# Features folded a second time on VectorE, and stage D in pairs of 64-row products: batches 2 to 7 of a Fourier and channel-mix kernel

## Chip, cores and metric

One core of a Trainium2 chip. The metric is the device time of one execution in microseconds (us); lower is better.

## What is computed

The input `x` has 8 batches of 3072 positions by 256 features, in float32.

```
X = fft over positions, then fft over features;  x = real part of X
x_prev = x one position earlier (zero at position 0)
xk = mu_k * x + (1 - mu_k) * x_prev
xr = mu_r * x + (1 - mu_r) * x_prev
k = relu(xk @ w_k) ** 2          # 256 -> 1024
r = sigmoid(xr @ w_r)            # 256 -> 256
out = r * (k @ w_v)              # 1024 -> 256, float32
```

## The kernel before

Everything is computed in float16 with float32 sums. A batch passes these stages.

- **Load and fold.** `load_xh` brings positions and mirrored positions into `xp` and `xm` (two halves h of a batch: 9 and 8 rows of 256 features on each partition). `fold` (L171, L173, VectorE) adds to each feature d the value at the mirrored place: `p`. `butterfly` (L182, VectorE) then adds and subtracts features 0 to 127 and 128 to 255 of `p`: `eo`, with an even part (e = 0) and an odd part (e = 1) of 128 features each.
- **Stage A** (`a_slots_0`, `a_half`; L553, L567): products of `eo` with a table of cosines and sines over part of the positions. The 48-row products come in pairs, one on the upper and one on the lower 64 rows of the array, and run side by side. Result `a`, features on partitions, copied from PSUM by ScalarE (L524).
- **Stage D** (`d_item`; L607): the transform over features. Each of 13 units takes two products of 128 rows and 128 columns (e = 0, 1) with the table `w_eo`; four units make an item, so a batch has three items of four units and one of one. The result goes to `g_all` by one copy for each item (`d_evac`, L524). `turned` (L630) multiplies column 128 of all units by a small table and writes it back.
- **Stage C** (`c_pairs`; L681): the rest of the transform over positions, in pairs of 64-row, 64-column products. Result `pq`. Four items a batch; in each batch the copy of the second one is made by VectorE (L522), the others by ScalarE.
- **Mixing** on VectorE: `halves` (L694) makes `y` from `pq`, `diff` (L702) the differences of neighbouring positions, `mix` (L714, L725) the inputs xk and xr.
- **Channel mix.** The positions of a batch are six chunks of 512. A chunk takes four steps. In each, `k_piece` makes four 512-column products (L760) and ScalarE the relu (L770, `rl`); every second step `square` (L780, VectorE) squares two steps' worth. `v_tile` (L801) multiplies with `w_v`, eight products a step, five steps behind the k products; its first four products read the square of the chunk's first half, its last four that of the second. `r_item` (L787, L792) comes once a chunk. `v_out` (L823, VectorE) multiplies by r, and SP's queue writes the result.

PSUM is six banks for three wide tiles (`ps_w`: psW, 1024 columns) and two for two narrow ones (`ps_v`: psV). Each wide product group takes the next of the three tiles in turn, and so must wait until the tile's last copy has been read out.

**Order.** The program is one list of 197 steps, written out by hand and pinned on every engine (`pin_order`). `at(step, ...)` puts work into a step, `event(step, ...)` puts a run of paired items right behind that step's v products. In a step PE issues the k products, the items of the step, the v products, and then the event. If an event has more than two items and does not begin with `a_slots_0`, the next step's v products are moved up to stand right behind it, ahead of the next step's k products (`early_v`, L925 to L930).

From step s0 = 24 b on (b = 0 to 5), batch t = b + 2 is prepared: folds and butterflies at s0 + 9 to 14, stage D items at s0 + 27, 29, 31 and 33, `turned` at s0 + 34, and three events at s0 + 37 (two C items and a stage A half item of batch t + 1), s0 + 41 (the same) and s0 + 45 (slot 0 and the last two stage A half items, which fill the two tiles that slot 0 has taken). For t = 7 there is no next batch and two events are left. A stretch below is one uninterrupted run of paired products. Batch 2's folds and butterflies stand earlier, at steps 17 to 21, beside the mixing of batch 1.

Of the kernel before, what the change touches and what calls it, by code (L numbers as in the profile page):

```python
# [10 lines left out]
FP16 = mybir.dt.float16  # L11
INT32 = mybir.dt.int32
UINT32 = mybir.dt.uint32
AF = mybir.ActivationFunctionType
ALU = mybir.AluOpType
# [5 lines left out]
def _v(ap, extra_offset, free_dims):  # L21
    new_ap = [list(ap.ap[0])] + [[s, c] for (s, c) in free_dims]
    return dataclasses.replace(ap, offset=ap.offset + extra_offset, ap=new_ap)
# [16 lines left out]
def kernel(  # L40
# [10 lines left out]
    nc = tc.nc  # L51

    B, S, D = x.shape
    F = moe_w_k.shape[1]
    P = 128
    N1, R = 48, 64
    NSL = 27
    NU = 26
    NJ, NJ1 = 14, 6

    const = ctx.enter_context(tc.tile_pool(name="const", bufs=1))
    p_pool = ctx.enter_context(tc.tile_pool(name="p", bufs=2))
    eo_pool = ctx.enter_context(tc.tile_pool(name="eo", bufs=2))
    y_pool = ctx.enter_context(tc.tile_pool(name="y_sb", bufs=1))
    mix_pool = ctx.enter_context(tc.tile_pool(name="mix", bufs=1))
# [7 lines left out]
    def ps_slot(kind, n, cols):  # L73
        k = ps_n[kind] % n
        ps_n[kind] += 1
        return psum.tile([P, cols], FP32, name=f"ps{kind}{k}", tag=f"ps{kind}{k}", bufs=1)

    def ps_w():
        return ps_slot("W", 3, 1024)
# [25 lines left out]
    xp_t, xm_t, p_t, eo_t = {}, {}, {}, {}  # L105
    V = nc.vector
# [2 lines left out]
    xp_sb = [const.tile([112, 9, 256], FP16, name=f"xp{n}") for n in range(3)]  # L109
    xm_00 = const.tile([96, 514], FP16)  # L110
    xp_00 = const.tile([96, 9, 256], FP16)
    xp_32 = const.tile([96, 5, 256], FP32)
    idx_4 = const.tile([96, 2], UINT32)
    idx_8 = const.tile([96, B, 2], UINT32)
# [10 lines left out]
    def parts(b):  # L125
        return 112 if b > 1 else 96
# [32 lines left out]
    def fold(b, h, q0=0, n=0):  # L159

        n = n or 9 - h
        if (b, h) not in p_t:
            p_t[b, h] = p_pool.tile([112, 9, 256], FP16, name="p")
        k = parts(b)
        p, xp, xm = p_t[b, h][0:k], xp_t[b, h][0:k], xm_t[b, h][0:k]
        o = XM0 + 256 * (8 - h - q0)
        if (b, h, q0) == (0, 0, 0):
            xm, o = xm_00, 1
        if (b, h) == (0, 0) and q0 < 5:
            xp = xp_32  # L170
        V.tensor_tensor(out=p[:, q0:q0 + n], in0=xp[:, q0:q0 + n],  # L171
                        in1=_v(xm, o + 256, [(-256, n), (-1, 256)]), op=ALU.add)
        V.tensor_tensor(out=p[:, q0:q0 + n, 0], in0=xp[:, q0:q0 + n, 0],  # L173
                          in1=_v(xm, o, [(-256, n)]), op=ALU.add)

    def butterfly(b, h, n=0):
        n = n or 9 - h
        eo_t[b, h] = eo_pool.tile([112, 9, 2, 128], FP16, name="eo")
        k = parts(b)
        p = p_t[b, h][0:k]  # L180
        for e in range(2):
            V.tensor_tensor(out=eo_t[b, h][0:k, 0:n, e], in0=p[:, 0:n, 0:128],  # L182
                            in1=p[:, 0:n, 128:256], op=ALU.subtract if e else ALU.add)
# [51 lines left out]
    for xm in xm_sb:  # L235
        V.memset(_v(xm, XM0 + 2048, [(256, 2)]), 0.0)
    V.memset(xm_00[:, 257:258], 0.0)
    iota = nc.gpsimd.iota
    def rows():
        for a in range(2):  # L240
# [7 lines left out]
    w_eo = const.tile([P, 2, 128], FP16)  # L248
    ramp = const.tile([P, P], INT32)
    row_i = const.tile([P, 4], UINT32)  # L250
    lo64, hi64 = slice(0, 64), slice(64, 128)
# [15 lines left out]
    g_all = const.tile([P, NU // 2, 256], FP16)  # L267
# [160 lines left out]
    def zero_rows():  # L428
        for n in (0, 2):
            nc.gpsimd.memset(xp_sb[n][32:64, 8], 0.0)  # L430
# [43 lines left out]
    def loads_2():  # L474
        for lo in (0, 64):
            k = slice(lo, 64 if lo == 0 else 112)
            iota(idx_g8[k], pattern=[[S // 8, B], [-1, 2]], base=S // 8 - 1 - lo // 16,
                 channel_multiplier=-8)
            iota(idx_g0[k], pattern=[[S, B]], base=S - lo // 2, channel_multiplier=-64)
        iota(idx_g0[0:1], pattern=[[S, B]], base=0, channel_multiplier=0)  # L480
        for a in range(2):
            gather(wk_sb[1][a], moe_w_k, row_i[:, 2 + a:3 + a])
        load_xh(1, 1)
        for a in range(2):
            gather(wr_sb[1][a], moe_w_r, row_i[:, 2 + a:3 + a])
        zero_rows()

    def eo_sine():
        nc.scalar.activation(out=w_eo.rearrange("p a b -> p (a b)"),
# [9 lines left out]
    def half_tables():  # L499
        ps = ps_w()  # L500
        turned(8, 13, ps, "")
        for o, w, step in ((512, 0, 2), (512, 1, 2), (512 + WB, WA, 1)):
            nc.tensor.matmul(out=ps[0:112, o:o + WB], lhsT=order[0:96, 0:112],
                             rhs=_v(w_pm[0:96], w, [(step, WB)]), start=w != 1, stop=w > 0)
        evac(_v(g_all, 256 * 8 + 128, [(256, 5)]), ps[:, 0:5], "A")
        V.tensor_copy(out=w_hh, in_=ps[0:112, 512:512 + 2 * WB])

    def eo_rest():

# [6 lines left out]
    a_t = {}  # L516
# [3 lines left out]
    def evac(out_ap, in_ap, eng):  # L520
        if eng == "V":
            V.tensor_copy(out=out_ap, in_=in_ap)  # L522
        else:
            nc.scalar.activation(out=out_ap, in_=in_ap, func=AF.Copy)  # L524
# [86 lines left out]
    def d_evac(ps, u0, n, bank, eng):  # L611
        evac(_v(g_all, 256 * u0, [(64, 2), (128, 2 * n), (1, 64)]),
             _v(ps, 0, [(bank, 2), (64, 2 * n), (1, 64)]), eng)

    def d_item(b, n, eng="A"):

        k = min(4, NU // 2 - 4 * n)
        ps = ps_w()
        d_units(b, ps, 4 * n, k, 512)
        d_evac(ps, 4 * n, k, 512, eng)  # L620

    def d_small(b, u, n, eng="A"):
        ps = ps_v()
# [223 lines left out]
    for a in range(2):  # L847
        nc.tensor.matmul(out=mu_ps[:, 2 * a:2 * a + 2], lhsT=mu_p[:, a], rhs=unit, start=True,
                         stop=True)
# [26 lines left out]
    w, first = ps_w(), ps_w()  # L876
# [15 lines left out]
    for a in range(2):  # L892
        t = x_t["t", a] = mix_pool.tile([P, 24, 64], FP16, name=f"t{a}")
        ts(t[:, 0:4], y[:, 0:4, a], mu_n[:, a, 0:1], MUL)
    for a in range(2):
        for z in range(2):
            V.scalar_tensor_tensor(out=_v(x_t[0, 0, 0], 1536 * a + 64 * z, [(128, 2), (1, 64)]),  # L897
                                   in0=_v(first, 512 + 64 * a - 384 * z, [(128, 2), (1, 64)]),
                                   scalar=mu_f[:, a, 0:1],
                                   in1=_v(x_t["t", a], 64 * z, [(128, 2), (1, 64)]),  # L900
                                   op0=ALU.mult, op1=ALU.add)
# [15 lines left out]
    work = {}  # L917

    def at(step, f, *args):
        work.setdefault((step, "x" if f in (a_item, a_sum, d_item, d_small, c_item, c_tiles, turned, minus_0, r_item) else "w"),  # L920
                        []).append((f, args))


# [3 lines left out]
    def event(step, *items):  # L927
        work.setdefault((step, "e"), []).extend((f[0], f[1:]) for f in items)
        if len(items) > 2 and items[0][0] is not a_slots_0:
            early_v.add(step + 1)  # L930
# [2 lines left out]
    nk = 4 * len(chunks)  # L933

    LAG, EARLY, SHORT = 5, 3, 3
    ES, EV = (37, 41, 45), "AVAAAAAA"
    OUT_FIRST = (12, 20, 28, 36, 38, 40)
    SQUARE_A = (6, 7, 8, 9)
    v_steps = {4 * n + tb + LAG: (c, tb) for n, c in enumerate(chunks) for tb in range(4)
# [61 lines left out]
    at(17, c_tiles, 1)  # L1001
    at(17, fold, 2, 0)
    event(18, (c_item, 1, 0, 8), (c_item, 1, 8, 8))
    at(18, butterfly, 2, 0)
    at(18, fold, 2, 1)
    event(20, (c_item, 1, 16, 8), (c_item, 1, 24, 4), (a_half, 2, 0, 0))
    at(19, diff, 1, 0, 12)
    at(20, r_item, (0, 1, 1))
    at(23, a_half, 2, 0, 1)
    at(20, mix, 1, 0, 0, 0, 0, 12)  # L1010
    at(21, butterfly, 2, 1)
    at(21, mix, 1, 0, 0, 1, 0, 12)
    at(22, diff, 1, 12, 26)
    at(21, load_gate)
# [6 lines left out]
    at(26, mix, 1, 0, 1, 0)  # L1021
    event(27, (a_slots_0, 2), (a_half, 2, 1, 0), (a_half, 2, 1, 1))
    at(28, r_item, (1, 0, 0))
    at(28, d_item, 2, 0)
    at(28, mix, 1, 0, 1, 1)
    at(29, d_item, 2, 1)
    at(30, mix, 1, 1, 1, 0)
    at(31, d_item, 2, 2)
    at(31, mix, 1, 1, 1, 1)
    at(32, r_item, (1, 0, 1))  # L1030
    at(33, d_item, 2, 3)
    at(34, turned, 0, 13)
    for n, c in enumerate(chunks[8:]):
        at(4 * n + 36, r_item, c)
    for b in range(B):
        s0 = 24 * b

        for n, st0 in enumerate((2, 4, 6, 8) if b > 1 else ()):
            at(s0 + st0, mix, b, n // 2, 1, n % 2)
        if b and b + 3 < B:  # L1040
            at(s0 + 22, load_gate)
            for h in range(2):
                at(s0 + 22, load_xh, b + 3, h)
        t = b + 2
        if t < B:
            if b:
                for n, st0 in enumerate((9, 10, 12, 14)):
                    at(s0 + st0, butterfly if n % 2 else fold, t, n // 2)
                for n, st0 in enumerate((27, 29, 31, 33)):
                    at(s0 + st0, d_item, t, n)  # L1050
                at(s0 + 34, turned, 0, 13)
            c = [(c_pairs, t, 8 * n, (8, 8, 8, 4)[n], EV[n]) for n in range(4)]
            if t + 1 < B:
                event(s0 + ES[0], c[0], c[1], (a_half, t + 1, 0, 0, EV[4]))
                event(s0 + ES[1], c[2], c[3], (a_half, t + 1, 0, 1, EV[5]))
                event(s0 + ES[2], (a_slots_0, t + 1), (a_half, t + 1, 1, 0, EV[6]), (a_half, t + 1, 1, 1, EV[7]))
            else:
                event(s0 + ES[0], *c[:2])
                event(s0 + ES[1], *c[2:])
        t = b + 1  # L1060
        if b and t < B:
            at(s0 + 16, halves, t, 0, 15)
            at(s0 + 18, halves, t, 15, 27)
            for a in range(2):
                at(s0 + 19 + a, diff, t, 0, 26, (a,))
                at(s0 + 21 + a, mix, t, 0, 0, a)
            at(s0 + 24, mix, t, 1, 0, 0)
            at(s0 + 25, mix, t, 1, 0, 1)
# [62 lines left out]
```

## Time and profile before

| | |
|---|---|
| median of 3 runs | 430.96 us (430.59 to 430.97) |
| the profiled execution, first to last instruction | 429.1 us |
| PE (TensorE) busy | 423.1 us |
| DVE (VectorE) busy | 360.2 us |
| ACT (ScalarE) busy | 321.0 us |
| POOL (GpSimd) busy | 65.5 us |

The span of the profiled execution is 1.9 us below the median: the profile counts from the first to the last instruction. Rows of the timeline give start, duration, engine, line, operation, operands and count; merged rows hold several instructions of one kind. PE's matmuls are pipelined and their ends are modelled, so the time that a group holds PE is read from its start to the start of the next group. Rows of groups end in busy time, mean of one in ns, and idle time before them with what ended it.

### The profile page before, as it was taken

Reading aid. Unit: us, or ns where it says so; the run is one execution under the profiler, and the core shown is the slowest. Engines: PE = TensorE matmul, PEld = TensorE weight load, DVE = VectorE, ACT = ScalarE, POOL = GpSimd, SP = SyncE. Lnnn points to the kernel's source line nnn. Section 1 sums busy time; section 2 is a strip of 40 time slices with the busy share of each in tenths; the row PEclk is TensorE's granted clock in tenths of the full one; section 3 lists DMA queues with packets and bytes.
Section 4 is the critical chain, followed back from the end, with each engine's and each line's share of the span. In section 5 each row is a group of like instructions: output and inputs, shape, how many; then the busy total and the mean of one; then the engine's idle time right before and its main releaser. Section 6 shows DMA issues by size and latency. Waiting matters only on the chain.

```text
span 429.1 us, 9294 instructions
## 1 busy us (share of the span) xinstructions
PE 423.1 (99%) x3855; PEld 298.7 (70%) x3855; DVE 360.2 (84%) x548; ACT 321.0 (75%) x374; POOL 65.5 (15%) x95
## 2 busy tenths in 40 slices
PE   8999999999999999999999999999999999999996
PEld 3767776777777766777777777677767767766765
DVE  8899999988998889988898988989799847997453
ACT  7889897877878687777777777777786767666661
POOL 7378602000050002300041000500000000000000
PEclk9999999999999999999999999999999999999999
DMA  8779956322385233932268222763222322223233
GB/s 172 107 104 205 230 129 128 75 66 58 75 154 140 56 72 66 197 90 66 63 111 190 54 58 68 140 153 72 59 70 50 76 67 59 70 64 72 67 74 98
DMA packets 35102, 42.06 MB, mean 98 GB/s; under 512 B 4114, under 2 KB 31092, under 8 KB 35060
## 3 DMA queue, kind: packets, MB, share of 16 engines
q1 hardware_dynamic: 27488, 25.41, 23.8%
q0 software_dynamic: 7264, 15.80, 22.2%
q8 instruction: 30, 0.49, 0.5%
q10 hardware_dynamic: 308, 0.26, 0.2%
q14 instruction: 12, 0.10, 0.1%
HBM read 32.08 MB, written 25.17 MB: 133 GB/s over the span
## 4 chain that ended last, share of the span: by engine, by line
PE 98%; DVE 1%; issue 0%; ACT 0%; POOL 0%
PE psW L760 39%; PE psV L801 37%; PE psW L787 10%; PE psV L813 3%; PE psW L607 3%; PE psW L681 1%; PE psW L567 1%; PE psW L206 1%; PE psW L585 1%; PE psW L649 1%; PE psV L347 1%; DVE rw L277 0%; PE psV L607 0%; PE psV L585 0%; PE psW L544 0%
## 5 line engine op out<-in xcount | busy, mean ns | idle before, releaser
L770 ACT ACTIVATE rl<-psW 128x1024 f16<-128x1024 f32 x192 | 195.0, 1025 | 91.5 <-PE psW L760 87.7
L760 PE MATMUL psW<-x,wk 128*128 128x512 f16 (+1 forms) x776 | 195.1, 377 | 0.3 <-DVE x L897 0.3
L801 PE MATMUL psV<-wv_sb,k 128*128 128x256 f16 x1424 | 184.1, 273 | 0.0
L801 PEld LDWEIGHTS <-k 128*128 128x128 f16 x1424 | 136.9, 98 | 35.6
L780 DVE TENSOR_TENSOR k<-rl 128x2048 f16<-128x2048 f16 (+1 forms) x100 | 115.6, 1156 | 33.6 <-ACT rl L770 33.2
L760 PEld LDWEIGHTS <-wk 128*128 128x128 f16 x776 | 74.9, 98 | 52.9 <-issue 0.4
L823 DVE SCALAR_TENSOR_TENSOR o<-psV,r 128x512 f32<-128x512 f32 (+1 forms) x97 | 65.7, 680 | 14.4 <-PE psV L801 13.0
L725 DVE TENSOR_TENSOR x<-y,t 128x1536 f16<-128x1536 f16 (+3 forms) x74 | 62.1, 845 | 2.1
L787 PE MATMUL psW<-wr,x 128*128 128x256 f16 x384 | 49.8, 273 | 0.0
L792 ACT ACTIVATE r<-psW 128x1024 f16<-128x1024 f32 x48 | 48.9, 1019 | 0.8 <-PE psW L787 0.8
L787 PEld LDWEIGHTS <-x 128*128 128x128 f16 x384 | 37.5, 98 | 14.3
L463 POOL IOTA gate<- 1x1 int32 x7 | 2.3, 323 | 200.4 <-DVE gate L462 200.4
L524 ACT ACTIVATE a<-psW 128x832 f16<-128x832 f32 x31 | 26.0, 863 | 1.8 <-PE psW L567 1.4
L524 ACT ACTIVATE g_all<-psW 128x1024 f16<-128x1024 f32 (+5 forms) x37 | 25.6, 694 | 0.3 <-PE psW L607 0.2
L140 POOL DMA_INDIRECT xm<-in_x_dram,idx_g x18 | 24.7, 1374 | 5.5 <-issue 5.5
L171 DVE TENSOR_TENSOR p<-xp,xm 112x2304 f16<-112x2304 f16 (+6 forms) x19 | 21.6, 1139 | 0.0
L714 DVE TENSOR_SCALAR t<-d,muf_t 128x1536 f16<-128x1536 f16 (+3 forms) x42 | 21.2, 517 | 0.1
L714 DVE TENSOR_SCALAR t<-d,mu_m 128x1536 f16<-128x1536 f16 x32 | 19.6, 613 | 0.0
L607 PEld LDWEIGHTS <-a 128*128 128x128 f16 x208 | 14.0, 98 | 6.5 <-ACT a L524 0.5
L182 DVE TENSOR_TENSOR eo<-p 112x1152 f16<-112x1152 f16 (+3 forms) x28 | 17.9, 678 | 0.0
L524 ACT ACTIVATE pq<-psW 128x1024 f16<-128x1024 f32 (+1 forms) x18 | 15.2, 880 | 2.3 <-PE psW L681 2.3
L702 DVE TENSOR_TENSOR d<-y 128x1664 f16<-128x1664 f16 (+5 forms) x19 | 16.7, 879 | 0.3 <-ACT y L524 0.3
(136 smaller groups left out, 219.9 us busy)
## 6 DMA issues: line engine op xcount, KB each, us to landing
out_dram<-o SPq DMA_DIRECT2D x189, 128.0 KB, 2.4
xp<-in_x_dram POOLq DMA_DIRECT2D x12, 216.0 KB, 4.7
xp<-in_x_dram POOLq DMA_DIRECT2D x13, 192.0 KB, 7.4
xp<-in_x_dram POOLq DMA_DIRECT2D x2, 384.0 KB, 6.7
wv_sb<-in_moe_w_v_dram POOLq DMA_DIRECT2D x1, 512.0 KB, 8.7
xp<-in_x_dram SPq DMA_DIRECT2D x1, 480.0 KB, 4.1
xp<-in_x_dram POOLq DMA_DIRECT2D x1, 432.0 KB
xm<-in_x_dram,idx_g POOLq DMA_INDIRECT x18, 8.2
```

The costliest lines, as they stand in the source:

```text
L140: nc.gpsimd.indirect_dma_start(dst, None, src, bass.IndirectOffsetOnAxis(ap=idx, axis=0))
L524: nc.scalar.activation(out=out_ap, in_=in_ap, func=AF.Copy)
L607: nc.tensor.matmul(out=ps[:, o:o + 128], lhsT=a_t[b][:, e, 2 * (u0 + i):2 * (u0 + i) + 2, :], rhs=w_eo[:, e], start=True, stop=True)
L714: V.tensor_scalar(out=dst, in0=src, scalar1=mu, scalar2=None, op0=ALU.mult)
L725: V.tensor_tensor(out=_v(x_t[b, j, m], o, [(64 * step, hi - lo), (step, 64)]), in0=y_t[b][:, lo + 3 * m:hi + 3 * m, a], in1=x_t["t", a][:, ...
L760: nc.tensor.matmul(out=st["k", ds][:, 512 * hs + lo:512 * hs + hi], lhsT=wk_sb[m][a][:, 128 * fc:128 * fc + 128], rhs=xk[:, a, 512 * i + l ...
L770: nc.scalar.activation(out=st["rl"][:, 2 * ds:2 * ds + 2], in_=st["k", ds].rearrange("p (f t) -> p f t", f=2), func=AF.Relu, bias=0.0, sca ...
L780: V.tensor_tensor(out=k2_t[c][:, lo:hi], in0=r, in1=r, op=ALU.mult)
L787: nc.tensor.matmul(out=ps[:, 256 * tb:256 * tb + 256], lhsT=x_t[b, 1, m][:, a, 512 * i + 128 * tb: 512 * i + 128 * tb + 128], rhs=wr_sb[m] ...
L792: nc.scalar.activation(out=st["r", c], in_=ps, func=AF.Sigmoid)
L801: nc.tensor.matmul(out=st["v", tb - h][:, 256 * h:256 * h + 256], lhsT=k2_t[c][:, fc, 128 * tb:128 * tb + 128], rhs=wv_sb[:, fc], start=(f ...
L823: V.scalar_tensor_tensor(out=o.rearrange("p a b -> p (a b)")[:, 0:256 * n], in0=st["v", t0][:, 0:256 * n], scalar=16.0, in1=st["r", c][:, ...
```

## The change

For batches 2 to 7 the butterfly becomes two functions. `quarters_1` makes sums of the two feature halves (128 features), their differences for features 0 to 63, and, reading backwards, differences for features 128 down to 65. `quarters_2` adds and subtracts these once more, so that each part e of `eo` holds two groups of 64 features, and sets two single features of each row from `p`. Stage D's products then need 64 rows each: `d_half` makes two products of 64 rows and 64 columns for each former one, one on the upper and one on the lower rows of the array, and copies in two operations of 512 columns, the first of which writes every second column. Its table `w_d` is made once in `quarter_tables`. `p` gets two fixed tiles, and a tile pool `t` is added for the intermediate result.

The order changes too. `turned` is split (units 0 to 11, unit 12). Twelve items of a batch, four of D, four of C and four of A, stand in four events at s0 + 29, 33, 41 and 45 (three for t = 7). All C items are copied by ScalarE.

```diff
+    def quarters_1(b, h):
+        n = 9 - h
+        t = eo_t[b, h, "t"] = t_pool.tile([112, 9, 256], FP16, name="t")
+        p = p_sb[h]
+
+        def half(o, q, step, w, op):
+            V.tensor_tensor(out=t[:, 0:n, o:o + w], in0=_v(p, q, [(256, n), (step, w)]),
+                            in1=_v(p, q + 128, [(256, n), (step, w)]), op=op)
+
+        half(0, 0, 1, 128, ALU.add)
+        half(128, 0, 1, 64, ALU.subtract)
+        half(192, 128, -1, 64, ALU.subtract)
+
+    def quarters_2(b, h):
...
+        def pairs(a, o, step, w=64):
+            return _v(a, o, [(256, n), (step, 2), (1, w)])
+
+        V.tensor_tensor(out=pairs(z, 0, 192), in0=pairs(t, 0, 128), in1=pairs(t, 64, 128),
+                        op=ALU.add)
+        V.tensor_tensor(out=pairs(z, 64, 64), in0=pairs(t, 64, 64), in1=pairs(t, 0, 192),
+                        op=ALU.subtract)
+        V.tensor_tensor(out=pairs(z, 128, 64, 1), in0=pairs(p, 0, 64, 1),
+                        in1=pairs(p, 128, 64, 1), op=ALU.subtract)
...
+    def quarter_rows():
+        iota(same_i, pattern=[[0, 2], [1, 64]], base=0, channel_multiplier=-1)
+        nc.gpsimd.tensor_scalar(out=same, in0=same_i, scalar1=0.0, scalar2=None,
+                                op0=ALU.is_equal)
+
+    def quarter_tables():
+        ps = ps_w()
+        nc.tensor.matmul(out=ps[:, 0:128], lhsT=same, rhs=w_eo[:, 1], start=True, stop=True)
+        for g, rows in enumerate((lo64, hi64)):
+            evac(w_d[rows, 0], _v(w_eo[rows], g, [(2, 64)]), "A")
+            evac(w_d[rows, 1], ps[rows, 64 * g:64 * g + 64], "A")
+        for k in range(2):
+            V.memset(_v(w_d[64:65], 64 + k, [(2, 32)]), 2.0 * k - 1.0)
...
+    def d_half(b, n, eng="A"):
+        u0, k = 4 * n, min(4, NU // 2 - 4 * n)
+        ps = ps_w()
+        for i in range(k):
+            for e in range(2):
+                for g, rows in enumerate((lo64, hi64)):
+                    o = 512 * g + 256 * e + 64 * i
+                    nc.tensor.matmul(out=ps[:, o:o + 64],
+                                     lhsT=a_t[b][rows, e, 2 * (u0 + i):2 * (u0 + i) + 2, :],
+                                     rhs=w_d[rows, e], start=True, stop=True)
+        evac(_v(g_all, 256 * u0, [(1, 2), (128, 2 * k), (2, 32)]),
+             _v(ps, 0, [(512, 2), (32, 2 * k), (1, 32)]), eng)
+        evac(_v(g_all, 256 * u0 + 64, [(128, 2), (256, k), (1, 64)]),
+             _v(ps, 256, [(512, 2), (64, k), (1, 64)]), eng)
...
-    ES, EV = (37, 41, 45), "AVAAAAAA"
+    EVENTS = (29, 33, 41, 45)
...
-            c = [(c_pairs, t, 8 * n, (8, 8, 8, 4)[n], EV[n]) for n in range(4)]
-            if t + 1 < B:
-                event(s0 + ES[0], c[0], c[1], (a_half, t + 1, 0, 0, EV[4]))
-                event(s0 + ES[1], c[2], c[3], (a_half, t + 1, 0, 1, EV[5]))
-                event(s0 + ES[2], (a_slots_0, t + 1), (a_half, t + 1, 1, 0, EV[6]), (a_half, t + 1, 1, 1, EV[7]))
-            else:
-                event(s0 + ES[0], *c[:2])
-                event(s0 + ES[1], *c[2:])
+            c = [(c_pairs, t, 8 * n, (8, 8, 8, 4)[n], "A") for n in range(4)]
+            d = [(d_half, t, n) for n in range(4)]
+            a = [(a_half, t + 1, h, e) for h in range(2) for e in range(2)] if t + 1 < B else []
+            at(s0 + 32, turned, 0, 12)
+            at(s0 + 37, turned, 12, 13)
+            event(s0 + EVENTS[0], *d[:3])
+            event(s0 + EVENTS[1], d[3], *c[:2])
+            event(s0 + EVENTS[2], *c[2:], *a[:1])
+            if a:
+                event(s0 + EVENTS[3], (a_slots_0, t + 1), a[2], a[3], a[1])
```

The features of batch 2 change in the same way at steps 17 to 22 (`quarters_1` in place of `butterfly` at 18 and 21, `quarters_2` at 19 and 22, `quarter_tables` at 22), those of batches 3 to 7 at s0 + 9 to 15.

More of the change, by code (lines that the diff above doesn't have):

```diff
@@ L61 @@
     const = ctx.enter_context(tc.tile_pool(name="const", bufs=1))
-    p_pool = ctx.enter_context(tc.tile_pool(name="p", bufs=2))
+    t_pool = ctx.enter_context(tc.tile_pool(name="t", bufs=1))
     eo_pool = ctx.enter_context(tc.tile_pool(name="eo", bufs=2))
@@ L111 @@
     xp_00 = const.tile([96, 9, 256], FP16)
+    p_sb = [const.tile([112, 256 * (9 - h) + 2], FP16, name=f"p{h}") for h in range(2)]
     xp_32 = const.tile([96, 5, 256], FP32)
@@ L162, in fold @@
         if (b, h) not in p_t:
-            p_t[b, h] = p_pool.tile([112, 9, 256], FP16, name="p")
+            p_t[b, h] = p_sb[h][:, 0:256 * (9 - h)].rearrange("p (q d) -> p q d", d=256)
         k = parts(b)
@@ L174, in fold @@
                           in1=_v(xm, o, [(-256, n)]), op=ALU.add)
+    def quarters_1(b, h):
[9 more added lines that the diff above has]
+    def quarters_2(b, h):
+        n = 9 - h
+        z = eo_t[b, h] = eo_pool.tile([112, 9, 2, 128], FP16, name="eo")
+        t, p = eo_t[b, h, "t"], p_sb[h]
+        def pairs(a, o, step, w=64):
[6 more added lines that the diff above has]
+                        in1=pairs(p, 128, 64, 1), op=ALU.subtract)
     def butterfly(b, h, n=0):
@@ L237 @@
     V.memset(xm_00[:, 257:258], 0.0)
+    for h, pt in enumerate(p_sb):
+        V.memset(pt[:, 256 * (9 - h):256 * (9 - h) + 2], 0.0)
     iota = nc.gpsimd.iota
@@ L486, in loads_2 @@
         zero_rows()
+        quarter_rows()
     def eo_sine():
@@ L506, in half_tables @@
         V.tensor_copy(out=w_hh, in_=ps[0:112, 512:512 + 2 * WB])
+    w_d = const.tile([P, 2, 64], FP16)
+    same_i = const.tile([P, P], INT32)
+    same = const.tile([P, P], FP16)
+    def quarter_rows():
[10 more added lines that the diff above has]
+            V.memset(_v(w_d[64:65], 64 + k, [(2, 32)]), 2.0 * k - 1.0)
     def eo_rest():
@@ L919, in at @@
     def at(step, f, *args):
-        work.setdefault((step, "x" if f in (a_item, a_sum, d_item, d_small, c_item, c_tiles, turned, minus_0, r_item) else "w"),
+        work.setdefault((step, "x" if f in (a_item, a_sum, d_item, d_small, c_item, c_tiles, turned, minus_0, r_item, quarter_tables) else "w"),
                         []).append((f, args))
@@ L1003 @@
     event(18, (c_item, 1, 0, 8), (c_item, 1, 8, 8))
-    at(18, butterfly, 2, 0)
+    at(18, quarters_1, 2, 0)
+    at(19, quarters_2, 2, 0)
     at(18, fold, 2, 1)
@@ L1010 @@
     at(20, mix, 1, 0, 0, 0, 0, 12)
-    at(21, butterfly, 2, 1)
+    at(21, quarters_1, 2, 1)
+    at(22, quarters_2, 2, 1)
     at(21, mix, 1, 0, 0, 1, 0, 12)
@@ L1023 @@
     at(28, r_item, (1, 0, 0))
-    at(28, d_item, 2, 0)
     at(28, mix, 1, 0, 1, 1)
-    at(29, d_item, 2, 1)
+    at(22, quarter_tables)
     at(30, mix, 1, 1, 1, 0)
-    at(31, d_item, 2, 2)
     at(31, mix, 1, 1, 1, 1)
     at(32, r_item, (1, 0, 1))
-    at(33, d_item, 2, 3)
-    at(34, turned, 0, 13)
     for n, c in enumerate(chunks[8:]):
@@ L1046 @@
             if b:
[L1047 to L1051, printed above, removed]
-            c = [(c_pairs, t, 8 * n, (8, 8, 8, 4)[n], EV[n]) for n in range(4)]
-            if t + 1 < B:
-                event(s0 + ES[0], c[0], c[1], (a_half, t + 1, 0, 0, EV[4]))
-                event(s0 + ES[1], c[2], c[3], (a_half, t + 1, 0, 1, EV[5]))
-                event(s0 + ES[2], (a_slots_0, t + 1), (a_half, t + 1, 1, 0, EV[6]), (a_half, t + 1, 1, 1, EV[7]))
-            else:
-                event(s0 + ES[0], *c[:2])
-                event(s0 + ES[1], *c[2:])
+                at(s0 + 9, fold, t, 0)
+                at(s0 + 10, quarters_1, t, 0)
+                at(s0 + 11, quarters_2, t, 0)
+                at(s0 + 12, fold, t, 1)
+                at(s0 + 14, quarters_1, t, 1)
+                at(s0 + 15, quarters_2, t, 1)
+            c = [(c_pairs, t, 8 * n, (8, 8, 8, 4)[n], "A") for n in range(4)]
[8 more added lines that the diff above has]
+                event(s0 + EVENTS[3], (a_slots_0, t + 1), a[2], a[3], a[1])
         t = b + 1
```

## The prediction

> **What bounds the kernel now.** I read the page's engine shares and chain first, then PE's timeline of one batch, then those of ACT and DVE beside it.
>
> ```profile
> span 429.1 us, 9294 instructions
> PE 423.1 (99%) x3855; PEld 298.7 (70%) x3855; DVE 360.2 (84%) x548; ACT 321.0 (75%) x374; POOL 65.5 (15%) x95
> PEclk9999999999999999999999999999999999999999
> PE 98%; DVE 1%; issue 0%; ACT 0%; POOL 0%
> ```
>
> PE carries 98% of the chain at full clock, so the time is what PE issues plus what PE waits. PE's ends are modelled, so I work from starts. Next is PE's timeline of one batch (start, duration, line, count).
>
> ```profile
> 199.21 1.04 PE L801 MATMUL psV<-wv_sb,k 128*128 128x256 f16 x8
> 200.18 0.64 PE L681 MATMUL psW<-m_cs,g_all 64*128 64x64 f16 x32
> 200.66 0.37 PE L567 MATMUL psW<-w_hh,eo 48*128 48x52 f16 x16
> 200.96 1.05 PE L801 MATMUL psV<-wv_sb,k 128*128 128x256 f16 x8
> ...
> 216.50 1.04 PE L801 MATMUL psV<-wv_sb,k 128*128 128x256 f16 x8
> 217.37 0.22 PE L553 MATMUL psW<-w_hh,eo 112*128 112x52 f16 x2
> 217.52 0.57 PE L567 MATMUL psW<-w_hh,eo 48*128 48x52 f16 x30
> 218.03 1.04 PE L760 MATMUL psW<-x,wk 128*128 128x512 f16 x4
> ...
> 228.46 0.61 PE L607 MATMUL psW<-w_eo,a 128*128 128x128 f16 x8
> 228.90 1.04 PE L801 MATMUL psV<-wv_sb,k 128*128 128x256 f16 x8
> ...
> 233.25 0.61 PE L607 MATMUL psW<-w_eo,a 128*128 128x128 f16 x8
> 233.70 0.49 PE L801 MATMUL psV<-wv_sb,k 128*128 128x256 f16 x3
> ...
> 243.81 0.19 PE L630 MATMUL psW<-g_all,turn 128*128 128x13 f16 x1
> 243.84 0.38 PE L801 MATMUL psV<-wv_sb,k 128*128 128x256 f16 x2
> ```
>
> Each row starts where the one before stops issuing: in this stage PE waits for nobody. What the change takes from PE is therefore worth its full length, and every new wait costs its full length.
>
> **The change part by part.** *Stage D's products.* The 8 of an item take 0.44 and 0.45, 0.0556 us each. A batch has 13 units, 26 products. They become 26 pairs of 64 rows and 64 columns, the form of L681: its 16 pairs take 200.18 to 200.66, 0.030 a pair. Six batches save 6 x 26 x (0.0556 - 0.030) = **4.0 us**.
>
> *One stretch more.* Eight L801 products take 0.87 (216.50 to 217.37). From 199.21 that ends at 200.08, but the pairs begin at 200.18: 0.10 to enter. Eight L567 pairs (about 0.025 each) end at 200.86, and L801 starts at 200.96: 0.10 to leave. The stage D items now stand in stretches too, and each batch has one stretch more (4 for 3, the last 3 for 2): 6 x 0.20 = **+1.2**. The turned product is split, one more of 0.03 (L630): **+0.2**. PE issues 2.6 us less.
>
> *The fourth item in the last stretch.* Four items take wide PSUM tiles there: both slot-0 products' tiles, which the half items of h = 1 fill, and now the half item of h = 0, e = 1. The ring has three. Call the tile of this step's k product A; the slot-0 tiles are B and C, the added item takes A, and the next k product needs B, whose copy is the first that ACT makes after the stretch. Before, it took A. No v product stands between, as the two v products moved ahead elsewhere do: the code makes that exception for a stretch that begins with the slot-0 products. ACT at that place, and the copies' forms:
>
> ```profile
> 216.70 1.02 ACT L770 ACTIVATE rl<-psW 128x1024 f16<-128x1024 f32 x1 [0.67 <-PE psW L760]
> 217.93 1.62 ACT L524 ACTIVATE a<-psW 128x832 f16<-128x832 f32 x2 [0.21 <-PE psW L567]
> ...
> L524 ACT ACTIVATE a<-psW 128x832 f16<-128x832 f32 x31 | 26.0, 863 | 1.8 <-PE psW L567 1.4 <-PE psW L585 0.4
> ```
>
> A is free (its rl copy ends at 217.72). B's copy runs 217.93 to 218.79, so k can start at about 218.84 (0.05 for the hand-over, an estimate from the 0.04 between the last L681 pair's result and ACT's start in the next fence). Without the wait k would start at 218.03 plus 8 more pairs, 218.23. PE waits 0.61, in the five batches with a next batch: **+3.05**. Nothing pays it back, since PE had no other wait to lose. Queued behind that k product are all of PE's later products; they move as one.
>
> *ACT in the first stretch.* Three D items stand together, each with two copies of 512 columns in place of one of 1024.
>
> ```profile
> 200.63 1.02 ACT L524 ACTIVATE pq<-psW 128x1024 f16<-128x1024 f32 x1 [0.19 <-PE psW L681]
> ...
> 209.33 1.51 ACT L524 ACTIVATE pq<-psW 128x1024 f16<-128x1024 f32 x2 [0.19 <-PE psW L681]
> 210.73 0.87 ACT L524 ACTIVATE a<-psW 128x832 f16<-128x832 f32 x1
> ...
> L489 ACT ACTIVATE w_eo<-ueo,sc 128x256 f16<-128x256 int32 x1 | 0.5, 491 | 0.0
> L399 ACT ACTIVATE w_pm<-u_w,sc 128x52 f16<-128x52 int32 x2 | 0.9, 435 | 0.0
> ```
>
> The pair of 1024 and 512 columns occupies ACT from 209.33 to 210.73, 1.40: 0.91 and 0.49. From the stretch's first pair (zero): ACT starts at 0.45, the second item's copies end at 0.45 + 3 x 0.49 + 0.60 = 2.52. The second k product after the stretch needs that tile: 24 pairs 0.72, leaving 0.10, v 0.87, k 0.87, so it would start at 2.56 and waits about 0.01 with the hand-over; the ends are this close. One of the two copies writes every second column of g_all, which no 512-column row does. Bounds: nothing; or 0.2 each, as L399, which also writes every second column, takes 435 where two scale operands and 52 columns leave 415 (L489 with one such operand gives 0.09 for it), 20 ns over 52 columns, times 512. I take 0.03 a copy, near the fixed end, as L399's excess is small in all: 0.1 a stretch, 6 x 0.1 = **+0.6**; at the far end it would be 0.45 a stretch, +2.7. The copy of c's second item goes from DVE to ACT (0.91 at a place where ACT idles 0.6 to 0.7 before each rl copy): no PE wait.
>
> *DVE.* A batch's features: two adds of 1152 and two of 1024 become six operations per half.
>
> ```profile
> 56.77 1.42 DVE L182 TENSOR_TENSOR eo<-p 112x1152 f16<-112x1152 f16 x2
> 58.10 1.22 DVE L171 TENSOR_TENSOR p<-xp,xm 112x2048 f16<-112x2048 f16 x1
> 59.36 0.20 DVE L173 TENSOR_TENSOR p<-xp,xm 112x8 f16<-112x8 f16 x1
> ...
> 61.01 1.22 DVE L780 TENSOR_TENSOR k<-rl 128x2048 f16<-128x2048 f16 x1
> ...
> 63.75 1.28 DVE L182 TENSOR_TENSOR eo<-p 112x1024 f16<-112x1024 f16 x2
> 64.95 0.41 DVE L714 TENSOR_SCALAR t<-d,muf_t 128x768 f16<-128x768 f16 x1
> ...
> 69.87 1.22 DVE L780 TENSOR_TENSOR k<-rl 128x2048 f16<-128x2048 f16 x1
> ...
> 78.83 1.22 DVE L780 TENSOR_TENSOR k<-rl 128x2048 f16<-128x2048 f16 x1
> ```
>
> Two of 1152 hold DVE 1.33 (56.77 to 58.10), 0.67 each, two of 1024 1.20: 0.55 ns a column and 0.04 fixed. So 576 columns 0.36, and the 18-element operation 0.23 (0.10 and a wait of 0.13, as 58.10's fold holds 1.26 before the small L173). Half 0: 3 x 0.67 + 2 x 0.36 + 0.23 = 2.96 for 1.33, half 1 2.7 for 1.2: 3.1 a batch more. In the steady batches the CAST below goes, with the idle time before it:
>
> ```profile
> 196.12 1.22 DVE L780 TENSOR_TENSOR k<-rl 128x2048 f16<-128x2048 f16 x1 [0.29 <-ACT rl L770]
> ...
> 200.87 1.23 DVE L522 CAST pq<-psW 128x1024 f16<-128x1024 f32 x1 [1.55 <-PE psW L681]
> ```
>
> 1.23 + 1.55 cover 2.8 of the 3.1. Half 0 comes ahead of that cover and makes the square at 196.12 1.63 - 0.29 = 1.3 late; it ends at 197.34 and is needed in the v row of 199.21, 0.44 into it, 2.3 later: no PE wait. Batch 2's features are made beside batch 1's mixing, where nothing goes. The squares (L780) there feed these v products (their last four products, 0.44 into a row, read the late square):
>
> ```profile
> 63.09 1.05 PE L801 MATMUL psV<-wv_sb,k 128*128 128x256 f16 x8
> ...
> 72.20 1.04 PE L801 MATMUL psV<-wv_sb,k 128*128 128x256 f16 x8
> ...
> 81.58 1.04 PE L801 MATMUL psV<-wv_sb,k 128*128 128x256 f16 x8
> ```
>
> The square at 61.01 ends at 62.23, 1.25 before 63.53 with the hand-over taken; it comes 1.55 later: PE waits 0.3. The next (71.09, needed at 72.64, 1.5 to spare) comes 1.55 + 1.5 + 0.15 (two small memsets) - 0.3 already waited - 0.3 of idle time = 2.6 late: PE waits 1.05. The third (80.05) is needed at 82.02, or 81.13, since two D items of 0.44 leave the steps ahead: 1.03 to spare, 1.5 late: 0.45. Sum **+1.8**; 0.8 if an operation costs a fifth less, 2.4 with the reversed read below.
>
> That read takes both inputs backwards from even columns. Folds read backwards at the full rate (2048 columns in 1.22, as squares), from odd columns, and this copy begins at an odd column:
>
> ```profile
> L656 DVE COPY g<-g_all x1: 189/189/189, 53.2 to 53.2; 128x127 f16<-128x127 f16 x1
> ```
>
> Its 189 ns leave no room for a slow rate, so I take the full one. The Trainium skill ("VectorE: DVE Perf Modes", section Mode 2×_1P) asks for 4-byte alignment before an operation gives two results a cycle, which these pairs lack; the Trainium skill ("Vector Engine (DVE) Microarchitecture Reference", section 5.1) reports that alignment made no difference. No row here shows a reversed, unaligned pair.
>
> POOL gets two small operations (15% busy), SP's queue keeps its order, no DMA is added. The products that make the new table are one of 128 columns and four small copies: under 0.1.
>
> **Sum.** -4.0 + 1.2 + 0.2 + 3.05 + 0.6 + 1.8 = +2.8: the profiled execution goes from 429.1 to 431.9. The median shown is 1.9 above the span (start and end, untouched): 430.96 + 2.8 = **433.8 us**.
>
> **Rivals.**
> - *Strided copies are slow*: 0.2 more each, 2.1 over the forecast, 435.9. For: L399's excess. Against: L399 is only 20 ns over.
> - *The reversed read runs at half rate*: 0.3 more per half. 0.6 more in batch 2's waits, 434.4; with the steady batches' cover of 2.8 against 3.7 then too thin in places, up to 436. By the first of the two pages of the Trainium skill this would be the case.
> - *Not slower: the ring lets k through.* If the k product behind the last stretch did not wait for B's copy, 3.05 goes: 430.7, no difference. It decides at 218.23: the copy would have to end within 0.30 of its start, where 31 rows say 0.86, or the tile would have to be another. For it speaks only that the ring is counted from the code; no row of before shows such a wait.
>
> **How the numbers follow.** About 0.2%, 0.9 us, can be told from no change. Forecast 0.60, slow copies 0.14, reversed read 0.16, ring free 0.10. The ring case divides between no difference and, if DVE too is less late, faster (0.04); 0.02 of the forecast falls within 0.2%. Slower 0.88, same 0.08, faster 0.04. Low end: DVE at 0.8 and the first stretch at nothing give 432.2, less 0.5 for a part of the ring case; high end: slow copies with some of the reversed read, 436.3.
>
> **What would show it.** In the changed profile: five PE gaps of about 0.6 ahead of a k product, released by an ACT copy of a, 50.8 apart; three waits of v products for squares near 63, 73 and 82, 1.8 in all; D pairs at 0.03; four stretches a batch; 512-column copies to g_all near 600 ns (800 for the slow-copy rival); the reversed 576 near 0.45 (0.75 for its rival). I am wrong if k does not wait there, or if the squares in batch 2 come in time.

## The result, and the profile after

| | before | after |
|---|---|---|
| median | 430.94 us (430.59 to 430.97, 4 runs) | 434.11 us (434.02 to 434.36, 4 runs) |
| ratio | | 1.0081 (95% interval 1.0067 to 1.0096) |
| span of the profiled execution | 429.1 us | 432.2 us |

The forecast was 433.8. First the page of the changed kernel, its share rows and its chain.

```profile
span 432.2 us, 9708 instructions
PE 421.7 (98%) x4018; PEld 294.5 (68%) x4018; DVE 371.3 (86%) x594; ACT 329.8 (76%) x414; POOL 62.3 (14%) x97
PE 88%; DVE 5%; ACT 4%; issue 1%; POOL 0%; POOLq 0%; DVEq 0%
```

PE is busy 1.4 us less in an execution 3.1 us longer, and the chain, 98% PE before, now runs 9% through DVE and ACT. The view of PE's waits names them (who waits, for whom; total, times, longest).

```profile
PE psW L825 <- ACT a L574: 2.8, 5, 0.6
PE psV L866 <- DVE k L845: 1.5, 3, 0.9
```

L825 is the k product (L760 before), L866 the v product (L801), L574 the copies on ACT (L524), L845 the square (L780), L679 the new pairs of stage D. The view counts idle time from modelled ends, so it comes out too short; I take the waits from starts, as in the prediction. PE and ACT at the last stretch of a batch:

```profile
117.04 0.21 PE L603 MATMUL psW<-w_hh,eo 112*128 112x52 f16 x2
117.19 0.77 PE L617 MATMUL psW<-w_hh,eo 48*128 48x52 f16 x46
118.52 1.02 PE L825 MATMUL psW<-x,wk 128*128 128x512 f16 x4 [0.55 <-ACT a L574]
```
```profile
117.60 2.38 ACT L574 ACTIVATE a<-psW 128x832 f16<-128x832 f32 x3 [0.21 <-PE psW L617]
```

In the kernel before, 30 of the paired products and the change back to 128-row products took 0.51 (L567 in the prediction), and 16 more take 0.2. So the k product would start at 117.90. It starts at 118.52, a wait of 0.62, five times: 3.1. It begins 0.06 after the first of the three copies of 0.86 has ended.

PE in the stage of batch 2, and two of the squares that it waits for:

```profile
62.56 0.61 PE L866 MATMUL psV<-wv_sb,k 128*128 128x256 f16 x4
63.39 0.61 PE L866 MATMUL psV<-wv_sb,k 128*128 128x256 f16 x4 [0.23 <-DVE k L845]
...
72.12 0.60 PE L866 MATMUL psV<-wv_sb,k 128*128 128x256 f16 x4
73.65 0.61 PE L866 MATMUL psV<-wv_sb,k 128*128 128x256 f16 x4 [0.93 <-DVE k L845]
...
81.70 0.60 PE L866 MATMUL psV<-wv_sb,k 128*128 128x256 f16 x4
82.61 0.61 PE L866 MATMUL psV<-wv_sb,k 128*128 128x256 f16 x4 [0.31 <-DVE k L845]
```
```profile
62.12 1.22 DVE L845 TENSOR_TENSOR k<-rl 128x2048 f16<-128x2048 f16 x1
...
72.37 1.22 DVE L845 TENSOR_TENSOR k<-rl 128x2048 f16<-128x2048 f16 x1
```

Three groups of eight v products are torn in two. Four products take 0.44, so the waits are 0.39, 1.09 and 0.47, 1.95 in all. The first two of the second halves begin 0.05 and 0.06 after a square has ended (63.34, 73.59).

The third place is the first stretch, where no row carries a release:

```profile
134.25 0.88 PE L679 MATMUL psW<-w_d,a 64*128 64x64 f16 x48
135.06 1.05 PE L866 MATMUL psV<-wv_sb,k 128*128 128x256 f16 x8
135.95 2.10 PE L825 MATMUL psW<-x,wk 128*128 128x512 f16 x8
137.88 1.04 PE L866 MATMUL psV<-wv_sb,k 128*128 128x256 f16 x8
```
```profile
134.70 3.36 ACT L574 ACTIVATE g_all<-psW 128x512 f16<-128x512 f32 x6 [0.19 <-PE psW L679]
```

48 products, 24 pairs, hold PE 0.81 with the 0.10 to leave: 0.030 a pair, as L681's rows had it. The eight k products that follow take 135.95 to 137.88, 1.93, where eight at 0.216 take 1.73: 0.20 is a wait inside the row, for a tile that the second D item's copies free: these end at 136.97, and the fifth of the k products starts at 137.02. The same happens in all six batches: 1.2 to 1.3. The six copies take 3.36, where the prediction has 6 x 0.49 plus the last one's 0.1, 3.05.

The start differs too: the first k products of full width begin at 21.27 before and at 20.70 after.

```profile
21.27 1.89 PE L760 MATMUL psW<-x,wk 128*128 128x512 f16 x8
```
```profile
20.70 1.89 PE L825 MATMUL psW<-x,wk 128*128 128x512 f16 x8
```

So the two profiled executions differ by 3.1 + 1.95 + 1.25 of waits, by -0.57 at the start, and by what PE issues less. The difference of the spans is 3.1, which leaves 2.6 for that last term; the length of a batch gives the same figure without this sum (below, under the reasons why the prediction was right).

### The profile page after: what moved, and what is told of

It reads as the page before. It is cut to its first block, busy times and chain, and to the rows that moved or that the text cites. A ratio compares the mean times of both kernels' runs of the same rounds, so it can differ in the third digit from the quotient of the medians.

```text
span 432.2 us, 9708 instructions
## 1 busy us (share of the span) xinstructions
PE 421.7 (98%) x4018; PEld 294.5 (68%) x4018; DVE 371.3 (86%) x594; ACT 329.8 (76%) x414; POOL 62.3 (14%) x97
## 4 chain that ended last, share of the span: by engine, by line
PE 88%; DVE 5%; ACT 4%; issue 1%; POOL 0%; POOLq 0%; DVEq 0%
PE psW L825 36%; PE psV L866 33%; PE psW L852 9%; PE psV L878 3%; ACT g_all L574 2%; PE psW L746 1%; DVE k L845 1%; ACT a L574 1%; PE psW L235 1%; PE psW L679 1%; DVE x L790 1%; DVE o L888 1%; PE psW L635 1%; DVE t L779 1%; PE psW L617 1%
## 5 line engine op out<-in xcount | busy, mean ns | idle before, releaser
L825 PE MATMUL psW<-x,wk 128*128 128x512 f16 (+1 forms) x776 | 194.9, 377 | 3.4 <-ACT a L574 2.8
L866 PE MATMUL psV<-wv_sb,k 128*128 128x256 f16 x1424 | 184.7, 273 | 1.5 <-DVE k L845 1.5
L866 PEld LDWEIGHTS <-k 128*128 128x128 f16 x1424 | 136.6, 98 | 41.9 <-DVE k L845 2.3
L845 DVE TENSOR_TENSOR k<-rl 128x2048 f16<-128x2048 f16 (+1 forms) x100 | 115.6, 1157 | 37.1 <-ACT rl L835 36.8
L825 PEld LDWEIGHTS <-wk 128*128 128x128 f16 x776 | 75.3, 98 | 58.4 <-issue 5.1
L574 ACT ACTIVATE g_all<-psW 128x512 f16<-128x512 f32 (+5 forms) x67 | 28.8, 513 | 2.0 <-PE psW L679 1.6
L574 ACT ACTIVATE a<-psW 128x832 f16<-128x832 f32 x31 | 25.5, 865 | 1.4 <-PE psW L617 1.2
L574 ACT ACTIVATE pq<-psW 128x1024 f16<-128x1024 f32 (+1 forms) x24 | 20.8, 922 | 1.2 <-PE psW L746 1.2
L141 POOL DMA_INDIRECT xm<-in_x_dram,idx_g x18 | 20.0, 1110 | 5.5 <-issue 5.2
L183 DVE TENSOR_TENSOR t<-p 112x576 f16<-112x576 f16 (+3 forms) x36 | 17.2, 533 | 0.0
L759 DVE TENSOR_TENSOR y<-pq 128x960 f16<-128x960 f16 (+1 forms) x24 | 13.5, 605 | 2.7 <-ACT pq L574 2.4
```

Source lines behind the costliest of these rows:

```text
L141: nc.gpsimd.indirect_dma_start(dst, None, src, bass.IndirectOffsetOnAxis(ap=idx, axis=0))
L825: nc.tensor.matmul(out=st["k", ds][:, 512 * hs + lo:512 * hs + hi], lhsT=wk_sb[m][a][:, 128 * fc:128 * fc + 128], rhs=xk[:, a, 512 * i + l ...
L845: V.tensor_tensor(out=k2_t[c][:, lo:hi], in0=r, in1=r, op=ALU.mult)
L866: nc.tensor.matmul(out=st["v", tb - h][:, 256 * h:256 * h + 256], lhsT=k2_t[c][:, fc, 128 * tb:128 * tb + 128], rhs=wv_sb[:, fc], start=(f ...
```

## The experiments

My theory is that of the prediction, with the price of the first stretch corrected: three waits on PE, each with one cause (the ring of three PSUM tiles, late squares in batch 2, slow copies), eat a saving of 2.6. The rival is that ACT and DVE are simply fuller, so that a wait which is taken away comes back at the next product. The first four runs share one set of runs of the kernel before, the last three another.

| run | median, us | runs | before, us | ratio (95% interval) |
|---|---|---|---|---|
| v_ahead | 431.22 | 11 | 430.89 | 1.0009 (1.0000 to 1.0018) |
| b2_butterfly | 432.18 | 5 | 430.89 | 1.0033 (1.0020 to 1.0047) |
| alt_read | 433.53 | 5 | 430.89 | 1.0061 (1.0048 to 1.0074) |
| before_fourth | 433.72 | 6 | 430.89 | 1.0063 (1.0050 to 1.0075) |
| v_alt | 429.70 | 11 | 430.66 | 0.9981 (0.9972 to 0.9990) |
| v_alt_sq23 | 429.16 | 5 | 430.66 | 0.9962 (0.9948 to 0.9975) |
| v_alt_old2 | 428.94 | 5 | 430.66 | 0.9961 (0.9947 to 0.9975) |

### v_ahead: cover for the last stretch

```diff
-        if len(items) > 2 and items[0][0] is not a_slots_0:
+        if len(items) > 2 and (len(items) > 3 or items[0][0] is not a_slots_0):
```

> The changed kernel, with the next step's v products moved up behind the last stretch, as they already are behind the other three. Theory (the waits seen on PE are the loss): the five waits of 0.61 for the copy of the first half item lie behind 0.87 of v products and go; 434.1 - 3.1 = 431.0. Rival (ACT and DVE carry more work in all, and a wait taken away comes back at the next k or v product): less than 1.0 comes back, 433.1 or more.

431.22, 2.9 below the changed kernel. Its PE timeline at the same stretch:

```profile
117.44 0.77 PE L617 MATMUL psW<-w_hh,eo 48*128 48x52 f16 x46
118.14 1.05 PE L866 MATMUL psV<-wv_sb,k 128*128 128x256 f16 x8
119.03 1.24 PE L825 MATMUL psW<-x,wk 128*128 128x512 f16 x5
```

The v products start at once and the k products right behind them: the copy has 0.87 more to end in. The wait does not come back elsewhere: the view of waits of this run has no k product that waits for a copy of a, and a batch is 0.62 shorter than in the changed kernel (below). The theory holds, the rival falls for this wait.

### before_fourth: the wait without the rest of the change

```diff
-                event(s0 + ES[1], c[2], c[3], (a_half, t + 1, 0, 1, EV[5]))
-                event(s0 + ES[2], (a_slots_0, t + 1), (a_half, t + 1, 1, 0, EV[6]), (a_half, t + 1, 1, 1, EV[7]))
+                event(s0 + ES[1], c[2], c[3])
+                event(s0 + ES[2], (a_slots_0, t + 1), (a_half, t + 1, 1, 0, EV[6]), (a_half, t + 1, 1, 1, EV[7]),
+                      (a_half, t + 1, 0, 1, EV[5]))
```

> The kernel before, with one edit: the stage A half item of h = 0, e = 1 goes from the second stretch to the end of the last, as in the changed kernel; no other part of the change. Theory (the ring of three tiles): five waits of 0.61 in front of a k product, released by ACT's copy of a; 430.9 + 3.1 = 434.0. Rival (the wait needs the changed kernel's fuller ACT): no wait, 430.9 to 431.2.

433.72: moving one item costs the kernel before 2.8 (2.2 to 3.2). Its timeline shows the wait of the changed kernel, without a single D pair or second fold:

```profile
115.96 0.77 PE L567 MATMUL psW<-w_hh,eo 48*128 48x52 f16 x46
117.28 1.02 PE L760 MATMUL psW<-x,wk 128*128 128x512 f16 x4 [0.55 <-ACT a L524]
```

115.96 + 0.71 is 116.67: 0.61 again. The edit also leaves the second stretch with two items, so that the next step's v products no longer move up behind it; a batch grows by 0.60 in all, so this adds nothing that can be seen. The cost is that of the ring's count at this place, and not of a fuller ACT.

### b2_butterfly: batch 2 without the second fold

```diff
-    at(18, quarters_1, 2, 0)
-    at(19, quarters_2, 2, 0)
+    at(18, butterfly, 2, 0)
...
-    at(21, quarters_1, 2, 1)
-    at(22, quarters_2, 2, 1)
+    at(21, butterfly, 2, 1)
```

> The changed kernel, with batch 2's six feature operations per half replaced by the two of before, so the second fold is left out for batch 2 and stage D there works on features folded once; all else stays. Theory: DVE's 3.1 more beside batch 1's mixing make three squares late; the three waits of v products near 63, 73 and 82 (1.95 together) go, 434.1 - 1.95 = 432.2. Rival (the squares are late because ACT's relu copies are late): the waits stay and so does the time, 434.0 or more.

432.18, as expected to 0.1. The kernel leaves out batch 2's second fold while its stage D still works as if it were there, so batch 2's values are not those of the task; only its time is used. The v products that were torn are whole:

```profile
62.59 1.05 PE L866 MATMUL psV<-wv_sb,k 128*128 128x256 f16 x8
...
71.75 1.04 PE L866 MATMUL psV<-wv_sb,k 128*128 128x256 f16 x8
...
80.23 1.04 PE L866 MATMUL psV<-wv_sb,k 128*128 128x256 f16 x8
```

All else of the change is still there, so the squares were late through DVE's added operations.

### alt_read: the D item's first copy written side by side

```diff
-        evac(_v(g_all, 256 * u0, [(1, 2), (128, 2 * k), (2, 32)]),
-             _v(ps, 0, [(512, 2), (32, 2 * k), (1, 32)]), eng)
+        evac(_v(g_all, 256 * u0, [(128, 2 * k), (2, 32), (1, 2)]),
+             _v(ps, 0, [(32, 2 * k), (1, 32), (512, 2)]), eng)
```

> The changed kernel; the first copy of a D item writes columns side by side and takes its inputs from the two PSUM halves in turn, in place of writing every second column. Theory (writing every second column costs 0.16 of the copy's 0.757): the copies fall to about 0.60, the waits of 0.216 behind the first stretch to 0.05 or less; 434.1 - 1.0 = 433.1. Rival (any copy that goes between two places column by column is slow): 0.75 or more again, 434.1 or more.

433.53, 0.6 below the changed kernel by the medians, 0.9 by the ratios, whose intervals overlap: the medians alone do not settle it. Of the two profiled executions this one starts late (first full-width products at 21.26); from there to the end it takes 410.5, the changed kernel from 20.70 on 411.5, and this is the 1.0 that was expected. The copies show the cause. First the changed kernel's six of one stretch (min/median/max ns), then five of this run's six:

```profile
L574 ACT ACTIVATE g_all<-psW x6: 589/698/780, 134.7 to 137.4; 128x512 f16<-128x512 f32 x6
```
```profile
L574 ACT ACTIVATE g_all<-psW x5: 592/606/632, 135.3 to 137.2; 128x512 f16<-128x512 f32 x5
```

And PE behind the stretch:

```profile
135.63 1.05 PE L866 MATMUL psV<-wv_sb,k 128*128 128x256 f16 x8
136.52 1.90 PE L825 MATMUL psW<-x,wk 128*128 128x512 f16 x8
138.25 1.04 PE L866 MATMUL psV<-wv_sb,k 128*128 128x256 f16 x8
```

Eight k products take 1.73 again: the wait is gone. The same edit on top of v_ahead (v_alt) is clear in the time as well: 1.0009 falls to 0.9981, 1.2 us.

### v_alt: both edits together

> v_ahead and alt_read together; the second fold stays in all six batches. Theory: the saving of 2.6 in PE's issuing is then set against the 1.95 of late squares in batch 2 alone: 430.9 - 0.65 = 430.3. Rival (the two waits cover for each other, and one is paid where the other goes): 431.0 or more.

429.70, with an interval just below 1: the change with two small edits is faster than the kernel before, by 0.8 (0.4 to 1.2), a fifth of a per cent. Of PE's waits past the start, one kind is left:

```profile
PE psV L866 <- DVE k L845: 1.4, 3, 0.9
```

It came out 0.6 below the 430.3 that was expected. 0.2 of this is the kernel before, whose median is 430.66 in this set and was 430.89 in the other. Its profiled execution starts early (20.68, against 21.27 before); from there to the end it takes 407.2 against 407.8, 0.6 less, and 0.65 was expected. Which start the other runs had isn't on record.

### v_alt_sq23: one square moved to ACT

```diff
-            square(chunks[step // 4], step % 4)
+            square(chunks[step // 4], step % 4, act=step in (23,))
```

> v_alt, with the square of step 23 on ACT, 1.2 less for DVE beside batch 1's mixing. Theory: the second wait for a late square (1.09) goes, the first (0.39) and most of the third (0.47) stay: 430.9 - 1.65 = 429.3. Rival (ACT has no room there and its relu copies come late in turn): a new wait of a k product takes its place, 430.3 or more.

429.16. The square takes ACT longer than DVE (1.91 for 1.22), and one of three waits goes:

```profile
70.11 1.91 ACT L843 ACTIVATE k<-rl 128x2048 f16<-128x2048 f16 x1
```
```profile
PE psV L866 <- DVE k L845: 0.5, 2, 0.3
```

From the first full-width products (21.21) to the end its profiled execution takes 406.2, 1.6 less than before's; 1.65 was expected. No new wait of a k product took its place, so the rival falls.

### v_alt_old2: batch 2 as before

Batch 2's features, D items and stretches are those of the kernel before, with its `turned` at step 34, and `quarter_tables` at step 35 (only the copy of its second C item stays on ACT); batches 3 to 7 as in v_alt.

```diff
+    at(28, d_item, 2, 0)
+    at(29, d_item, 2, 1)
+    at(31, d_item, 2, 2)
+    at(33, d_item, 2, 3)
...
+            if not b:
+                event(37, c[0], c[1], a[0])
+                event(41, c[2], c[3], a[2 - 1])
+                event(45, (a_slots_0, t + 1), a[2], a[3])
+                continue
```

> v_alt, with batch 2 left as in the kernel before (folded once, stage D in 128-row products, three stretches); batches 3 to 7 as changed. Theory: no wait on PE is left, and five sixths of the saving of 2.6 show in the time: 430.9 - 2.15 = 428.8. Rival (the pairs save less than their cadence says, or the cost of the stretches was taken too low): between 429.5 and 430.9.

428.94 (0.9961, 0.9947 to 0.9975), 1.7 below before, where five sixths of 2.6 are 2.15, within the interval (1.1 to 2.3). No v product waits for a square and no k product for a copy in its view of waits. By starts, though, one square is late:

```profile
97.48 1.22 DVE L845 TENSOR_TENSOR k<-rl 128x2048 f16<-128x2048 f16 x1
98.14 1.22 PE L866 MATMUL psV<-wv_sb,k 128*128 128x256 f16 x8
```

The square ends at 98.70 and the fifth of these v products starts at 98.75, where four at 0.11 would have let it start at 98.58: a wait of 0.17. Ahead of the square stand batch 3's second fold and the two memsets of `quarter_tables`, for which DVE waits 0.99, so step 35 was not a free place for it. Another 0.37 is lost in this execution near 52.5, where a product of batch 1's stage D waits for DVE's copy to `g_all`; v_alt loses nothing there and v_ahead 0.24, although their code is the same at that place. The two make up most of what is missing from 2.15. The saving in PE's issuing is real. v_alt_sq23 and this version can't be told apart.

## Why the prediction was right

- **PE issues 2.6 less.** Right. The new pairs hold PE 0.030 each, and the length of a batch shows the net saving free of the start and of batch 2. These are the first products of a last stretch and of the one two batches later, before, after and in v_alt:

```profile
166.66 0.21 PE L553 MATMUL psW<-w_hh,eo 112*128 112x52 f16 x2
268.08 0.21 PE L553 MATMUL psW<-w_hh,eo 112*128 112x52 f16 x2
...
168.13 0.22 PE L603 MATMUL psW<-w_hh,eo 112*128 112x52 f16 x2
270.32 0.21 PE L603 MATMUL psW<-w_hh,eo 112*128 112x52 f16 x2
...
167.05 0.21 PE L603 MATMUL psW<-w_hh,eo 112*128 112x52 f16 x2
267.60 0.21 PE L603 MATMUL psW<-w_hh,eo 112*128 112x52 f16 x2
```

  Half of each distance is the length of one batch: 50.71 before, 51.10 after (the prediction has 50.8) and 50.28 in v_alt, where neither of the steady batches' two waits is left: 0.43 less than before, 2.6 in six batches. Read in the same way, a batch takes 50.48 in v_ahead (0.62 less than after, the fourth item), 50.88 in alt_read (0.2 less, the first stretch) and 51.31 in before_fourth (0.60 more than before).
- **The fourth item in the last stretch, 3.05.** Right, in place, cause and size: 0.62 five times, taken away by cover (2.9) and brought to the kernel before by one moved item (2.8).
- **Batch 2's squares, 1.8.** Right: 0.39, 1.09, 0.47 for 0.3, 1.05, 0.45. The steady batches of the changed kernel show no such wait in the view, as said. The reversed read ran at the full rate, which ends that rival. The three operations of one half (min/median/max ns):

```profile
L183 DVE TENSOR_TENSOR t<-p x3: 451/462/752, 56.2 to 57.3; 112x576 f16<-112x576 f16 x2, 112x1152 f16<-112x1152 f16 x1
```

  The forward and the reversed 576 columns took 451 and 462.
- **ACT in the first stretch, 0.6: the term that was mis-sized.** It measured 1.2 to 1.3. The step that failed took 0.03 for a copy that writes every second column. The changed kernel's 18 such copies of 512 columns took 742 to 793 ns, its 18 that write side by side 580 to 658. That is about 0.15 for the strided write, near the far end of 0.2. From one start to the next, which is what PE waits for, the strided copies of the stretch shown take 0.59 to 0.61 and the others 0.47, where the prediction has 0.49 for both. So the four copies up to the end of the second item take 2.27 for 2.07, and this is the wait of 0.20. I had read L399's excess as a fixed cost of 20 ns rather than one for each column. The slow-copy rival was thus nearly true of the copy, while of its 2.1 only 0.65 came: 0.45 behind each stretch was expected of it, and 0.20 was there.
- **The start was not in the sum.** The changed kernel's profiled execution began its full work 0.57 earlier. All nine profiles here have that point at 20.7 or at 21.2 to 21.3, and the seven kernels with the changed start have both: after, v_ahead, b2_butterfly and v_alt 20.7, alt_read, v_alt_sq23 and v_alt_old2 21.2 to 21.3. So the change alone does not make it. The traces show what goes with it: PE's first products, of a tile of zeros, follow each other every 0.43 at first and every 0.22 later, and go over at 6.7 to 8.1 in the four early ones, at 8.8 or later in four of the five late ones. The fifth, before_fourth, goes over at 7.2 but makes the third of its first folds 0.6 later than before does. Two profiles without the change, both late, are too few to say that it has no part in the start at all. Without the 0.57 the terms make 3.7, so in the profiled executions the forecast is as near as it is partly by luck: two misses of 0.6 have opposite signs. For the medians this stays open, as the start of the other executions isn't on record; the interval of the ratio, 2.9 to 4.1, holds both 3.1 and 3.7.

## What to carry to other kernels

Where the engine that bounds the time never waits, read what a change takes from it at full length, and then count, at every place the change touches, how many buffers stand between it and the copy that frees the next one: one item too many in a ring of three cost more here (3.1) than the whole change saved in PE's issuing (2.6), and one moved group of products gave nearly all of it back. Added work on an engine with idle time is free only in stages that have that idle time; look for the stage that has none (here batch 2's) before the steady state. A layout that made a copy write every second element had a price of its own here, and reading alternately instead did not.

## What was not expected of the hardware

An ACT copy of 512 columns from PSUM that writes every second 16-bit column took 0.74 to 0.79 (0.58 to 0.66 when written side by side, both in the changed kernel; 0.60 to 0.63 in alt_read, where it reads from two PSUM halves in turn and writes side by side). The first full-width products begin at 20.7 or at 21.2 to 21.3 us, also among kernels whose program is the same up to there, and this goes with the moment at which PE's first products speed up from one every 0.43 us to one every 0.22 us (at 6.7 us in v_ahead, after 9.05 us in alt_read); what sets that moment stays open.
